# Linear attention and a mixture of experts in one kernel: the running state enters the key-value products through an identity matmul

## The chip, the cores and the metric

One core of one Trainium2 chip. The metric is the device time of one execution in microseconds (us). The kernel before takes 488.33 us in the median of three runs.

## The reference

For 4 sequences of 768 tokens and 8 heads of 48, a gated linear attention runs token by token: the state S of 48 x 48 is scaled row-wise by alpha and gets the outer product of k and v; the output is q times S. The 384 outputs of a token go through one of 8 experts (384 to 1024 to 384). Which one depends on a gate: a token takes its own best expert, or keeps that of the token before it.

```python
state = alpha[:, :, t, :, None] * state + np.einsum('bhd,bhe->bhde', k[:, :, t], v[:, :, t])
y[:, :, t] = np.einsum('bhd,bhde->bhe', q[:, :, t], state)
...
fresh_e = int(np.argmax(logits[b, s]))
e = fresh_e if (s == 0 or local_gate[b, s] < 0.5) else prev_e
h = np.maximum(x[b, s] @ w1[e], 0.0)
out[b, s] = p[e] * (h @ w2[e])
```

All is float32. The expert products split each operand into a high and a low part and add three products of one pass each (float32r).

## The kernel before, in words

**Attention in slots.** The tokens make 24 blocks of 128 (two chunks of 64), six for each of the 4 sequences; block i belongs to sequence i % 4. The main loop (L684) has a slot for each block and two slots more. In slot i the pieces of several blocks are issued, and the order of the program is kept on every engine (`pinned`, L658), so that what stands in the code is the order of each queue:

- `one_a(i+2)` and `scan2(i+1)`: GpSimd sets four ones in a; VectorE scans a backwards (tile sf), GpSimd scales k by it (x<-x,sf).
- `kt(i)`: TensorE transposes k (kp), ScalarE copies it (kk). `copies(i-1)`: ScalarE copies the states of both chunks (st) into the padded tile sb. `state(i-1)`: VectorE makes the next block's state of that sequence.
- `pm(i)`: 16 small products of k and q (pe); VectorE masks them (pq).
- `scan1(i+2)`: VectorE scans a forwards (A), GpSimd scales q by it (x<-x,A). Then the loads of a and x for block i+3 on SP.
- `xt(i-2)`: transposes the outputs (xp, copy xx) for the router. `ym(i-1)`: outputs from pq and v, and from q and sb (y), copy XR, store to xd; then `load_v(i+2)`.
- `first_v(i+1)`: ScalarE copies the first chunk's values beside a block of zeros in vt, so that one product gives both chunks' key-value sums.
- `um(i)`: eight products of kk and vt (up, four heads' pairs on two column groups); VectorE adds the state to both chunks' sums, PSUM to SBUF (L387). For the first four blocks the state is filled with zeros by GpSimd (L375).

Three times in a slot `other()` (L622) runs the deferred VectorE work, one step of each router that is under way, and either two products of zeros (`dense(DN)`, tile dz into h) or, once the first three groups are routed, a piece of the early experts' work.

**Routing** (`route`, L432) takes four blocks as a group when they are done. It is a generator: each `yield` ends a step, and an `other()` takes one step. Its pieces on TensorE are lg, lt, rp, rb, pw and lp; between them are small VectorE operations and ScalarE copies. The one-hot of a token's place in a tile (on) is made by eight ScalarE activations, in four steps; for the last group by VectorE at once.

**Experts.** When group 2 has been routed, `early()` (L562) gives out pieces: experts 0 and 1 for the first 1536 tokens, then the rest of expert 1. A piece is a transposition of gathered rows (tp, xh, xl), one first-layer tile (nine products into h, then hh on ScalarE and hl on VectorE; two halves of h2 alternate), or some second-layer products (yp). The weights of experts 0 and 1 are split by ScalarE (w1h, w2h) and VectorE (w1l, w2l) inside the slots. After the slots the remaining jobs run one after the other.

Setup (L647 to L657) fills constants on GpSimd ahead of the first block; further constants come three a slot from the list `made` (L660).

Of the kernel before, what the change touches and what calls it, by code (L numbers as in the profile page):

```python
# [8 lines left out]
F32 = mybir.dt.float32  # L9
# [10 lines left out]
DM = H * D  # L20
# [26 lines left out]
DN = 2  # L47
# [19 lines left out]
def gla_moe(ctx, tc, akq, vw, vn, wg, w1, w2, cst, tok, out):  # L67
# [188 lines left out]
    with ExitStack() as ac, ExitStack() as aa:  # L256
# [16 lines left out]
        for j in range(2):  # L273
            sb = ap.tile([R, 2, 2, CW], F32, bufs=1, name=f"sb{j}")
            g_.memset(sb[0:64], 0.0)
            g_.memset(sb[64:112, :, 1, :], 0.0)
            SBs.append(sb)
            oh = ap.tile([128, E, G + 1], F32, bufs=1, name=f"oh{j}")
            g_.memset(oh, 0.0)
            OHs.append(oh)  # L280

        st = {"c": c0}
        sts = [ap.tile([R, 3, HP, D], F32, tag="st", bufs=G + 1, name=f"st_{i}") for i in range(G)]
# [30 lines left out]

        def first_v(i):
            vt = VTs[i % NP]
            s_.copy(vt[0:64, 0, :], vt[0:64, 1, :])

        def scan1(i):
# [7 lines left out]
            q2 = x[:, BW:].rearrange("p (s t) -> p s t", t=C)  # L327
            g_.tensor_tensor(q2, q2, A.rearrange("p (s t) -> p s t", t=C + 1)[:, :, 1:], ALU.mult)
            d["k"] = x[:, 0:BW].rearrange("p (h t) -> p h t", h=HP)
            d["q"] = x[:, BW:2 * BW].rearrange("p (h t) -> p h t", h=HP)  # L330

# [37 lines left out]
        def um(i):  # L369
# [3 lines left out]
            if i < G:  # L373
                s3 = sts[i]
                g_.memset(s3[:, 0], 0.0)  # L375
            else:
                s3 = st["S", i % G]
            uw = pp.tile([128, 512], F32, tag="up", name=f"up_{i}")
            up = uw[0:R, 0:2 * CW].rearrange("p (h c d) -> p c h d", c=2, h=HP)
            for hp in range(HP):  # L380
                n = slice(2 * hp * D, 2 * (hp + 1) * D)
                t_.matmul(uw[64:112, n], lhsT=kk[:, hp, 64:112], rhs=vt[:, :, 2 * hp * D:(2 * hp + 1) * D],
                          start=True, stop=True)
                t_.matmul(uw[0:64, n], lhsT=kk[:, hp, 0:64], rhs=vt[:, :, (2 * hp + 1) * D:(2 * hp + 2) * D],
                          start=True, stop=True)
            n = 2 if i + G < NB else 1
            v_.tensor_tensor(s3[:, 1:1 + n], up[:, 0:n], s3[:, 0].unsqueeze(1).broadcast_to([R, n, HP, D]), ALU.add)  # L387
            d["s3"] = s3

        def copies(i):  # L390
            sf, sb = blk[i]["s3"].rearrange("p c h d -> p c (h d)"), blk[i]["sb"]
            s_.copy(sb[64:112, :, 0, :], sf[64:112, 0:2])
            s_.copy(sb[0:48, :, 1, :], sf[0:48, 0:2])

        def state(i):
            d = blk[i]
            if i + G < NB:
                sn = ap.tile([R, 3, HP, D], F32, tag="st", bufs=G + 1, name=f"st_{i + G}")
                v_.scalar_tensor_tensor(sn[:, 0], d["s3"][:, 2], 1.0 / SEED,
# [32 lines left out]
        def route(g):  # L432
# [36 lines left out]
            yield  # L469
# [29 lines left out]
            yield  # L499
            v_.tensor_tensor(ex, ex, ob, ALU.mult)  # L500
            pn = rt([128, n], "pn")
            v_.tensor_reduce(pn, ex, AX.X, ALU.add)
            v_.tensor_tensor(pl[:, :, 0], pn, se, ALU.mult)
# [5 lines left out]
            yield  # L509
            ps = rt([128, E, n + 1], "ps")  # L510
# [25 lines left out]
            if end:  # L536
                v_.tensor_tensor(on, iob.unsqueeze(1).broadcast_to([128, n, TS]),
                                 rr.unsqueeze(2).broadcast_to([128, n, TS]), ALU.is_equal)
            else:
                for j in range(n):  # L540
                    s_.activation(on[:, j], iob, AF.Abs, bias=rr[:, j:j + 1], scale=-1.0)
                    s_.activation(on[:, j], on[:, j], AF.Relu, bias=one[:, 0:1], scale=-float(TS))
                    if j < n - 1:
                        yield
# [17 lines left out]
        def early():  # L562
# [10 lines left out]
            for _ in range(4):  # L573
                yield False
# [47 lines left out]
        def other(pieces=True):  # L622
# [5 lines left out]
            if work[0] is None:  # L628
                if DN:
                    dense(DN)  # L630
# [46 lines left out]
        ]  # L677
        one_a(0)
        scan1(0)
        scan2(0)  # L680
        one_a(1)
        scan1(1)
        wsteps = iter(())
# [257 lines left out]
```

## Time and profile before

| what | us |
|---|---|
| three runs | 485.93, 488.33, 488.93 |
| profiled execution | 484.0 |
| its span | 482.2 |
| first key transposes (slot 0) | at 11.25 |
| slot 5, slot 12, slot 17 begin | at 40.63, 88.96, 119.94 |
| first product of the second early job | at 201.30 |

PE is TensorE's products, PEld its weight loads, DVE VectorE, ACT ScalarE, POOL GpSimd, SP the queue that issues most loads. The granted clock is 1.0 at full speed; its mean is 0.961. Nearly every instruction passes through a helper at line 81, so groups are told apart by tile names, not by lines. A float32 product leaves two records, a float32r product or a transposition one.

### The profile page before, as it was taken

What the parts mean: (1) busy time and instruction counts of PE and PEld (TensorE: products, weight loads), DVE (VectorE), ACT (ScalarE), POOL (GpSimd) and SP (SyncE); (2) the same over time, 40 slices, a digit from 0 to 9 for tenths busy, and PEclk for the clock granted to TensorE, in tenths of its full rate; (3) what the DMA queues carried; (4) which work ended last, traced back from release to release, by engine and by line L of the source; (5) the groups of instructions that cost most, each with busy time, mean ns of one, the idle gap of its engine ahead of it and who ended that gap; (6) DMA issues with size and microseconds to landing.
All of it is one profiled execution on the core that took longest, in us unless ns stands there. A gap on an engine that the chain in (4) does not pass through costs nothing.

```text
span 482.2 us, 10873 instructions
## 1 busy us (share of the span) xinstructions
PE 437.9 (91%) x4443; PEld 391.5 (81%) x4443; DVE 257.3 (53%) x485; ACT 194.1 (40%) x390; POOL 186.7 (39%) x207
## 2 busy tenths in 40 slices
PE   5999898999997978698989999999999999999990
PEld 5777776878875877597878998998989989989990
DVE  4778999898997235722274445244254252342310
ACT  1345656565756436321354324335144233242210
POOL 6654326364556000261053642724732503504201
PEclk9799999999998899888899999999999999999997
DMA  8789767596661102660075554444351542531100
GB/s 217 199 260 252 222 187 201 164 292 167 189 208 50 51 17 71 180 186 27 1 224 188 134 181 138 124 131 123 114 175 57 158 130 65 174 98 39 50 3 27
DMA packets 26710, 66.01 MB, mean 137 GB/s; under 512 B 4384, under 2 KB 10677, under 8 KB 26658
## 3 DMA queue, kind: packets, MB, share of 16 engines
q1 hardware_dynamic: 18672, 49.65, 36.3%
q0 software_dynamic: 3840, 10.62, 6.9%
q10 hardware_dynamic: 4146, 5.03, 3.1%
q8 instruction: 35, 0.57, 0.5%
q14 instruction: 17, 0.14, 0.1%
HBM read 55.84 MB, written 10.62 MB: 138 GB/s over the span
## 4 chain that ended last, share of the span: by engine, by line
PE 53%; issue 11%; DVE 9%; ACT 3%; POOL 2%; POOLq 0%; DVEq 0%; ACTq 0%
PE h L81 24%; PE yp L81 20%; PE y L81 3%; PE tp L81 2%; DVE A L81 2%; POOL out L81 1%; PE up L81 1%; DVE st L81 1%; DVE sf L81 1%; DVE pq L81 1%; ACT hh L81 1%; POOL w1l_0b L81 1%; PE pe L81 1%; DVE xl L81 1%; PE lp L81 1%
## 5 line engine op out<-in xcount | busy, mean ns | idle before, releaser
L81 DVE SCALAR_TENSOR_TENSOR hl<-h,hh 128x480 fp32r<-128x480 f32 (+2 forms) x80 | 43.9, 556 | 77.2 <-ACT hh L81 76.9
L81 ACT ACTIVATE hh<-h 128x480 fp32r<-128x480 f32 (+2 forms) x80 | 38.7, 490 | 82.4 <-PE h L81 82.3
L81 POOL DMA_INDIRECT out<-yo,idx x32 | 32.5, 1017 | 80.5 <-DVE yo L81 78.0
L81 POOL DMA_INDIRECT xg<-xd,idx x32 | 32.6, 1018 | 61.0 <-PE tp L81 52.9
L81 DVE TENSOR_SCALAR yo<-yp,acc 128x384 f32<-128x384 f32 (+1 forms) x32 | 19.6, 616 | 61.1 <-PE yp L81 61.0
L81 POOL TENSOR_TENSOR x<-x,sf 112x512 f32<-112x512 f32 x24 | 29.0, 1209 | 42.5 <-DVE sf L81 42.5
L81 POOL TENSOR_TENSOR x<-x,A 112x512 f32<-112x512 f32 x24 | 31.8, 1327 | 29.0 <-DVE A L81 6.6
L81 DVE TENSOR_TENSOR_SCAN A<-a,z 112x520 f32<-112x520 f32 x24 | 34.5, 1437 | 5.6 <-POOL a L81 5.6
L81 PE MATMUL h<-dz 128*128 128x256 f32 x142 | 35.0, 354 | 2.1 <-DVE z L81 2.1
L81 DVE TENSOR_TENSOR_SCAN sf<-a,z 112x520 f32<-112x520 f32 x24 | 33.8, 1408 | 0.1
L81 ACT COPY sb<-st 48x384 f32<-48x384 f32 x48 | 24.5, 510 | 11.5 <-DVE st L81 10.9
L81 PEld LDWEIGHTS h<-dz 128*128 128x128 f32 x142 | 23.8, 224 | 6.5 <-DVE z L81 2.1
L81 PEld LDWEIGHTS y<-vt,pq 64*64 64x64 f32 x768 | 24.9, 138 | 4.0 <-issue 3.8
L81 PE MATMUL y<-vt,pq 64*64 64x48 f32 x768 | 27.9, 224 | 0.0
L81 PE MATMUL y<-sb,x 112*64 112x96 f32 x384 | 21.8, 258 | 4.3 <-ACT sb L81 4.2
L81 PE MATMUL up<-vt,kk 128*48 128x96 f32 (+1 forms) x384 | 23.1, 267 | 0.0
L81 PEld LDWEIGHTS y<-sb,x 112*64 112x64 f32 x384 | 17.2, 140 | 6.2 <-ACT sb L81 5.2
L81 PEld LDWEIGHTS up<-vt,kk 128*48 128x48 f32 (+1 forms) x384 | 18.3, 140 | 3.4 <-issue 1.0
L81 ACT COPY kk<-kp 128x448 f32<-128x448 f32 x24 | 12.8, 531 | 20.7 <-PE kp L81 20.6
L81 PE MATMUL h<-xh,w1h_1a 128*128 128x256 f32 (+1 forms) x48 | 16.4, 342 | 3.9 <-DVE hl L81 2.7
L81 ACT COPY XR<-y 128x384 f32<-128x384 f32 x24 | 11.5, 479 | 20.1 <-PE y L81 20.1
L81 ACT CAST xh<-tp 128x384 fp32r<-128x384 f32 (+1 forms) x32 | 14.0, 462 | 13.9 <-PE tp L81 13.6
(247 smaller groups left out, 1234.8 us busy)
## 6 DMA issues: line engine op xcount, KB each, us to landing
x<-akq SPq DMA_DIRECT2D x24, 448.0 KB, 5.6
a<-akq SPq DMA_DIRECT2D x24, 227.9 KB, 4.5
vt<-vn SPq DMA_DIRECT2D x24, 192.0 KB, 2.7
xd<-XR ACTq DMA_DIRECT2D x24, 192.0 KB, 4.8
rw_0a<-w SPq DMA_DIRECT2D x3, 512.0 KB, 4.9
rw_0a<-w SPq DMA_DIRECT2D x4, 384.0 KB, 4.2
rw_1a<-w SPq DMA_DIRECT2D x3, 512.0 KB, 5.9
rw_1a<-w SPq DMA_DIRECT2D x4, 384.0 KB, 3.5
```

The costliest lines, as they stand in the source:

```text
L81: r = f(*a, **k)
```

## The change

- The state addition on VectorE goes. For blocks from the fifth on, `um` begins with a product of the identity and the state, repeated for both chunks (112 x 112 by 384 columns, float32), and the eight key-value products add to it in the same bank. `copies` takes the first chunk's state from SBUF and the second's straight from PSUM, four copies for two; `state` reads the third from PSUM. The state tiles shrink to a third.
- `first_v` goes; `load_v` loads the first chunk's values a second time, to where the copy put them.
- `copies` and `state` stand ahead of `kt` in a slot.
- Routing: one empty step goes, the product with the chosen expert (eo) goes to GpSimd, two VectorE operations move a step on, and the one-hot is made by VectorE in one operation for all groups: 11 steps for 15.
- Zeros: `other()` issues one product by default and two at its first call in a slot, four a slot for six. `early()` waits two calls instead of four between gather and transposition.
- Setup: of the fills ahead of the first block five stay on GpSimd; the rest go into `made`, five a slot. The scaling of q of block 0 stands behind that of k. c0 and c1 are worked out from ioa.

```diff
-DN = 2
+DN = 1
...
-        sts = [ap.tile([R, 3, HP, D], F32, tag="st", bufs=G + 1, name=f"st_{i}") for i in range(G)]
+        sts = [ap.tile([R, HP, D], F32, tag="st", bufs=G + 1, name=f"st_{i}") for i in range(G)]
...
-        def first_v(i):
-            vt = VTs[i % NP]
-            s_.copy(vt[0:64, 0, :], vt[0:64, 1, :])
+            y_.dma_start(VTs[i % NP][0:64, 0, :], vn[0:64, at * DM:(at + 1) * DM])
...
-            g_.tensor_tensor(q2, q2, A.rearrange("p (s t) -> p s t", t=C + 1)[:, :, 1:], ALU.mult)
+            d["A"] = A
+            if i:
+                scale_q(i)
...
+        def scale_q(i):
+            q2 = blk[i]["x"][:, BW:].rearrange("p (s t) -> p s t", t=C)
+            g_.tensor_tensor(q2, q2, blk[i].pop("A").rearrange("p (s t) -> p s t", t=C + 1)[:, :, 1:], ALU.mult)
...
-            if i < G:
-                s3 = sts[i]
-                g_.memset(s3[:, 0], 0.0)
-            else:
-                s3 = st["S", i % G]
             uw = pp.tile([128, 512], F32, tag="up", name=f"up_{i}")
             up = uw[0:R, 0:2 * CW].rearrange("p (h c d) -> p c h d", c=2, h=HP)
+            if i < G:
+                st["S", i] = sts[i]
+                g_.memset(sts[i], 0.0)
+            else:
+                t_.matmul(uw[0:R, 0:2 * CW], lhsT=ident[0:R, 0:R],
+                          rhs=st["S", i % G].unsqueeze(2).broadcast_to([R, HP, 2, D]), start=True, stop=False,
+                          skip_group_check=True)
...
-                          start=True, stop=True)
+                          start=i < G, stop=True, skip_group_check=True)
-            n = 2 if i + G < NB else 1
-            v_.tensor_tensor(s3[:, 1:1 + n], up[:, 0:n], s3[:, 0].unsqueeze(1).broadcast_to([R, n, HP, D]), ALU.add)
-            d["s3"] = s3
+            d["up"], d["S"] = up, st["S", i % G]
...
-            s_.copy(sb[64:112, :, 0, :], sf[64:112, 0:2])
-            s_.copy(sb[0:48, :, 1, :], sf[0:48, 0:2])
+            for c, x in ((0, d["S"]), (1, d["up"][:, 0])):
+                s_.copy(sb[64:112, c, 0], x[64:112])
+                s_.copy(sb[0:48, c, 1], x[0:48])
...
-                v_.scalar_tensor_tensor(sn[:, 0], d["s3"][:, 2], 1.0 / SEED,
+                v_.scalar_tensor_tensor(sn, d["up"][:, 1], 1.0 / SEED,
                                         d["end"].unsqueeze(2).broadcast_to([R, HP, D]), ALU.mult, ALU.mult)
...
-            yield
-            v_.tensor_tensor(ex, ex, ob, ALU.mult)
-            pn = rt([128, n], "pn")
-            v_.tensor_reduce(pn, ex, AX.X, ALU.add)
-            v_.tensor_tensor(pl[:, :, 0], pn, se, ALU.mult)
+            eo = rt([128, n, 8], "eo")
+            g_.tensor_tensor(eo, ex, ob, ALU.mult)
...
+            pn = rt([128, n], "pn")
+            v_.tensor_reduce(pn, eo, AX.X, ALU.add)
+            v_.tensor_tensor(pl[:, :, 0], pn, se, ALU.mult)
...
-            if end:
-                v_.tensor_tensor(on, iob.unsqueeze(1).broadcast_to([128, n, TS]),
-                                 rr.unsqueeze(2).broadcast_to([128, n, TS]), ALU.is_equal)
-            else:
-                for j in range(n):
-                    s_.activation(on[:, j], iob, AF.Abs, bias=rr[:, j:j + 1], scale=-1.0)
-                    s_.activation(on[:, j], on[:, j], AF.Relu, bias=one[:, 0:1], scale=-float(TS))
-                    if j < n - 1:
-                        yield
+            v_.tensor_tensor(on, iob.unsqueeze(1).broadcast_to([128, n, TS]),
+                                              rr.unsqueeze(2).broadcast_to([128, n, TS]), ALU.is_equal)
...
-            for _ in range(4):
-                yield False
+            yield False
+            yield False
...
-            if i < NB:
-                kt(i)
             if 0 < i <= NB:
                 copies(i - 1)
                 state(i - 1)
             if i < NB:
+                kt(i)
+            if i < NB:
                 pm(i)
...
-            for _ in range(min(3, len(made))):
+            for _ in range(min(5, len(made))):
                 made.pop(0)()
-            other(i >= NB)
+            other(i >= NB, 2)
```

On TensorE, slot 4 (the first with a state to add; cs holds the identity, h<-dz are zeros), before:

```order
L81 MATMUL kp_562<-cs,x_310 128x112 x4
L81 MATMUL pe_573<-x_310 64x64 x16
L81 MATMUL h_118<-dz 128x256 x2
L81 MATMUL xp_602<-cs,XR_538 128x128 x3
L81 MATMUL y_607<-vt_98,pq_493 64x48 x16
L81 MATMUL y_607<-sb_109,x_247 64x96 x8
L81 MATMUL h_118<-dz 128x256 x2
L81 MATMUL up_639<-vt_100,kk_567 48x96
L81 MATMUL up_639<-vt_100,kk_567 64x96
```

and now:

```order
L81 MATMUL kp_545<-cs,x_288 128x112 x4
L81 MATMUL pe_552<-x_288 64x64 x16
L81 MATMUL h_114<-dz 128x256 x2
L81 MATMUL xp_586<-cs,XR_518 128x128 x3
L81 MATMUL y_591<-vt_98,pq_471 64x48 x16
L81 MATMUL y_591<-sb_108,x_225 64x96 x8
L81 MATMUL h_114<-dz 128x256
L81 MATMUL up_622<-st_247,cs 112x384
L81 MATMUL up_622<-vt_100,kk_550 48x96
```

One product of zeros behind y is gone (and one behind up), and the identity product with its 384 columns stands ahead of the eight of up.

On VectorE, slot 6 (the pass from one pq to the next; w1l is the low part of a first-layer weight), before:

```order
L81 TENSOR_TENSOR pq_683<-pe_666,cs 128x512
L81 SCALAR_TENSOR_TENSOR A_687<-a_598,z_91 112x520
L81 RECIPROCAL z_92<-A_687 112x4
L81 TENSOR_TENSOR w1l_0a_731<-rw_0a_440,w1h_0a_730 128x1024
L81 TENSOR_TENSOR st_370<-up_751,st_370 112x384
L81 SCALAR_TENSOR_TENSOR sf_768<-a_598,z_92 112x520
L81 SCALAR_TENSOR_TENSOR st_780<-st_370,A_500 112x192
L81 TENSOR_TENSOR pq_799<-pe_782,cs 128x512
```

and now:

```order
L81 TENSOR_TENSOR pq_667<-pe_650,cs 128x512
L81 SCALAR_TENSOR_TENSOR A_673<-a_582,z_91 112x520
L81 RECIPROCAL z_92<-A_673 112x4
L81 TENSOR_TENSOR w1l_0a_717<-rw_0a_419,w1h_0a_716 128x1024
L81 SCALAR_TENSOR_TENSOR sf_752<-a_582,z_92 112x520
L81 SCALAR_TENSOR_TENSOR st_759<-up_736,A_480 112x192
L81 TENSOR_TENSOR pq_785<-pe_768,cs 128x512
```

The addition ahead of the backward scan is gone; the scaling behind the scan reads the bank up itself.

On TensorE, slot 20 behind the transposes of the outputs (pw is routing, w1h and w1l are expert 0's weights), before:

```order
L81 MATMUL y_2448<-vt_100,pq_2327 64x48 x16
L81 MATMUL y_2448<-sb_109,x_1984 64x96 x8
L81 MATMUL pw_2478<-oi_2391,one 128x40
L81 MATMUL pw_2478<-oh_112,trif 128x8x4
L81 MATMUL up_2481<-vt_102,kk_2406 48x96
```

and now:

```order
L81 MATMUL y_2444<-sb_108,x_1977 64x96 x8
L81 MATMUL h_114<-xh_0_2352,w1h_0a_716 128x256
L81 MATMUL h_114<-xl_0_2353,w1h_0a_716 128x256
L81 MATMUL h_114<-xh_0_2352,w1l_0a_717 128x256
L81 MATMUL h_114<-xh_0_2352,w1h_0a_848 128x256
L81 MATMUL h_114<-xl_0_2353,w1h_0a_848 128x256
L81 MATMUL h_114<-xh_0_2352,w1l_0a_849 128x256
L81 MATMUL h_114<-xh_0_2352,w1h_0a_958 128x256
L81 MATMUL h_114<-xl_0_2353,w1h_0a_958 128x256
L81 MATMUL h_114<-xh_0_2352,w1l_0a_959 128x256
L81 MATMUL up_2490<-st_2044,cs 112x384
```

The first tile of the first early job stands in slot 20 now; before, its place was slot 22. Over the whole program TensorE has 142 products of zeros before and 99 now.

51 lines of the change are left out of this document (26 added, 25 removed).

## The prediction

> **What bounds the kernel now.** I read the page first: busy shares of the engines and the row of the granted clock.
>
> ```profile
> span 482.2 us, 10873 instructions
> PE 437.9 (91%) x4443; PEld 391.5 (81%) x4443; DVE 257.3 (53%) x485; ACT 194.1 (40%) x390; POOL 186.7 (39%) x207
> DVE  4778999898997235722274445244254252342310
> PEclk9799999999998899888899999999999999999997
> ```
>
> TensorE is busy 91% of the span, but part of that is zeros, and the shares mix stages. VectorE's digits are 7 to 9 up to the fourteenth slice and low afterwards. So I cut the span where the program changes: the fill, slots 0 to 4, 5 to 11 (the first expert's weights are split here), 12 to 16, 17 up to the second early job's first product, and the rest. Columns are window, its length, busy time of PE, PEld, DVE, ACT, POOL, the clock, DMA share and GB/s.
>
> ```profile
> 0.00:11.25 11.25, 6.41 (x32) 6.20 (x33) 4.68 (x7) 1.80 (x2) 7.78 (x39) 0.98 0.88 213
> 11.25:40.63 29.38, 27.02 (x492) 22.60 (x493) 23.25 (x32) 12.23 (x25) 15.89 (x28) 0.89 0.85 240
> 40.63:88.96 48.33, 43.41 (x833) 36.27 (x832) 43.43 (x82) 29.74 (x66) 21.51 (x24) 0.96 0.68 196
> 88.96:119.94 30.98, 30.20 (x591) 25.48 (x590) 28.27 (x62) 18.64 (x45) 14.28 (x15) 1.00 0.77 226
> 119.94:201.30 81.36, 68.59 (x1045) 58.39 (x1044) 54.22 (x135) 43.70 (x104) 25.51 (x26) 0.96 0.37 107
> 201.30:250.00 48.70, 42.82 (x260) 39.75 (x260) 17.91 (x36) 13.04 (x27) 17.21 (x17) 0.86 0.35 105
> 250.00:482.20 232.20, 219.45 (x1201) 202.82 (x1199) 85.51 (x134) 74.91 (x122) 84.54 (x59) 0.98 0.38 113
> ```
>
> In slots 5 to 16 TensorE and VectorE are both near 90% or more (43.41 and 43.43 of 48.33; 30.20 and 28.27 of 30.98): neither can be relieved alone. In the fifth window TensorE is idle for 12.8 us, so there is time to win. After 250 us nothing of the change is left; I leave 232.2 us as they are.
>
> Idle time is not TensorE's only loss. Four stretches ran at half clock:
>
> ```profile
> 59.50:62.50 3.00, 3.00 (x42) 2.55 (x43) 2.30 (x6) 1.21 (x3) 1.23 (x2) 0.57 0.85 247
> 154.30:161.10 6.80, 6.80 (x71) 6.07 (x69) 1.33 (x8) 2.74 (x7) 1.79 (x2) 0.50 0.20 61
> 202.10:208.90 6.80, 6.08 (x29) 5.61 (x28) 2.38 (x7) 1.15 (x3) 4.83 (x5) 0.51 0.84 245
> 226.10:232.90 6.80, 5.93 (x26) 5.46 (x27) 1.03 (x3) 0.71 (x2) 0.00 (x0) 0.51 0.03 8
> ```
>
> Each costs about half its length where TensorE is the bound: 1.5, 3.4, 3.1 and 3.0 us. These rows show what TensorE waits for (first two columns: start and duration; the bracket is the idle time before):
>
> ```profile
> 151.68 0.53 DVE L81 TENSOR_TENSOR xl<-tp,xh 128x384 fp32r<-128x384 f32 x1
> 152.31 0.57 PE L81 MATMUL kp<-cs,x 112*128 112x112 f32 x4 [1.86 <-issue]
> 169.84 0.38 PE L81 MATMUL h<-xh,w1h_0a 128*128 128x256 f32 x1 [0.78 <-DVE hl L81]
> 192.16 0.22 PE L81 MATMUL rb<-cs,em 32*128 32x32 f32 x1 [1.58 <-DVE em L81]
> 200.42 1.10 PE L81 MATMUL lp<-vo,on 128*128 128x96 f32 x8 [2.50 <-DVE on L81]
> ```
>
> The 1.86 us "issue" ends as VectorE's xl frees the bank that kp needs. All of them wait, at the end, for VectorE: a queue of small work there holds TensorE up, although VectorE's average is only 53%. The closings of the clock follow such waits.
>
> **The change part by part.** Durations of what goes, stays and comes:
>
> ```profile
> L81 DVE TENSOR_TENSOR st<-up,st 112x384 f32<-112x384 f32 x20 | 10.9, 547 | 7.2 <-POOL a L81 3.8 <-PE up L81 1.8 <-POOL st L81 1.5
> L81 DVE TENSOR_TENSOR ex<-ex,oh 128x32 f32<-128x32 f32 x6 | 2.8, 466 | 0.0
> 199.59 0.68 DVE L81 TENSOR_TENSOR on<-iob,rr 128x512 f32<-128x512 f32 x1
> L81 ACT COPY vt<-vt 64x384 f32<-64x384 f32 x24 | 12.3, 512 | 12.3 <-ACT XR L81 8.5 <-DMA vt<-vn 3.9
> L81 ACT ACTIVATE on<-on,one 128x128 f32<-128x128 f32 x20 | 8.0, 402 | 0.6
> L81 ACT COPY sb<-st 48x384 f32<-48x384 f32 x48 | 24.5, 510 | 11.5 <-DVE st L81 10.9
> ```
>
> VectorE loses the state additions (10.9 us for twenty, shorter ones for the last four blocks) and six products with ex (2.8, now on GpSimd); it gains five one-hots of 0.68 us (3.4). Net some -0.5 us a slot. It also loses a place in its queue: the addition waited for um of the same slot and stood ahead of the backward scan, while now only the scaling of the state waits, behind the scan. That scaling now waits for ScalarE's copies too, as both read the same bank; queued behind it on VectorE are pq, for which the next slot's y waits, and the next A, for which GpSimd's scaling of q waits. The backward scan (1.2 us) ahead of it covers the two copies out of the bank. ScalarE loses 12.3 us of copies and 16 us of activations, and its 48 copies become 96 of half the width; by 0.51 us for 384 columns and 0.40 for 128 I take 0.3 to 0.43 each, so +4 to +17 us. It is 60% busy in slots 5 to 16, its copies start as um ends and the first two need no product at all, so I cost this at nothing; were the cover gone, 4 x 0.4 us ahead of kk would hold the transposes xp by about 0.6 us a slot. The second load of the values is 98 KB a block, 24 times, one more issue on SP behind load_v's wait for ym; um needs it two slots later, and DMA stands at 0.68 to 0.85. At nothing, with 1 us against me in slots 0 to 4, where it stands ahead of the next blocks' a and x on SP's queue.
>
> TensorE loses 43 products of zeros (the order of its instructions has 142 before, 99 after) and gains 20 products of 112x112 by 384 columns. The price of one zero product, by slots with the same routing (16 has six, 20 none):
>
> ```profile
> 114.17 0.55 PE L81 MATMUL kp<-cs,x 112*128 112x112 f32 x4
> 119.94 0.45 PE L81 MATMUL kp<-cs,x 112*128 112x112 f32 x3
> 137.09 0.60 PE L81 MATMUL kp<-cs,x 112*128 112x112 f32 x4
> 142.53 0.60 PE L81 MATMUL kp<-cs,x 112*128 112x112 f32 x4 [0.35 <-POOL x L81]
> 2.15 6.41 PE L81 MATMUL h<-dz 128*128 128x256 f32 x32 [2.15 <-DVE z L81]
> ```
>
> 119.94 - 114.17 = 5.77 against 5.44 - 0.35 = 5.09: 0.68 us for six, 0.11 each; the thirty-two at the start take 0.20 each. I take 0.13, nearer to the slots: 43 x 0.13 = 5.6 us (4.7 to 8.6).
>
> The identity product does not occur in the trace. Neighbours in float32 are
>
> ```profile
> L81 PE MATMUL y<-vt,pq 64*64 64x48 f32 x768 | 27.9, 224 | 0.0
> L81 PE MATMUL lg<-xx,wgs 128*32 128x128 f32 x144 | 6.8, 279 | 1.1 <-ACT xx L81 0.9
> 105.46 1.13 PE L81 MATMUL lp<-vo,on 128*128 128x96 f32 x8
> 106.37 0.37 PE L81 MATMUL h<-dz 128*128 128x256 f32 x1
> ```
>
> From 48 to 128 columns one record grows by 55 ns, 0.69 ns a column, and one product leaves two records: 384 columns stream in 0.53 us. That is the low end. The high end is four lp products, which also make 384 columns but load weights four times: 106.37 - 105.46 = 0.91 us. I take 0.70, between them, since weights are loaded once: 20 x 0.70 = +14.0 us (10.6 to 18.2). By the Trainium skill, FP8 and Floating Point Precision (TensorE Precision Notes), true float32 takes four passes; at the warm N / 2.4 of TensorE: Matmul & The Clock Gate (Back-to-back issue gap) that would be an estimate of 0.64 us and a term of 12.8 us.
>
> So TensorE has 14.0 - 5.6 = 8.4 us more to do, and only saved waits can make the kernel faster. By stage:
>
> Start, slots 0 to 4: -2.2. The a-memset of block 0 no longer stands behind 28 other fills, and the scaling of q is put behind that of k.
>
> ```profile
> 6.34 1.24 DVE L81 TENSOR_TENSOR_SCAN A<-a,z 112x520 f32<-112x520 f32 x1 [4.23 <-POOL a L81]
> 7.83 2.11 DVE L81 TENSOR_TENSOR_SCAN sf<-a,z 112x520 f32<-112x520 f32 x1
> 30.57 0.56 DVE L81 TENSOR_TENSOR st<-up,st 112x384 f32<-112x384 f32 x1 [1.28 <-POOL a L81]
> ```
>
> The first scan waits 4.23 us, but its data land only shortly before, and then pe waits for q: I take -0.7 (0 to -2). In slots 1 to 4 the state addition waits 1.28 us for the fill of the state, queued behind q's scaling; after it follow sf, the scaling, pq and the next A. Now the fill holds up ScalarE's copies instead and the scan goes ahead: about 0.4 us a slot, -1.5 (-2.5 to +1).
>
> Slots 5 to 11: fourteen zeros less, -1.8; seven identities, +4.9; idle 4.9 to 2.0 with VectorE 3.5 us lighter, -2.9; half of the first closing, -0.8. Sum -0.6. Slots 12 to 16: eleven zeros less, -1.4, five identities, +3.5, next to no idle time to win, -0.2: +1.9.
>
> Slot 17 to 201.30: eight zeros less, -1.0; seven identities, +4.9; lp of the third group, now over by slot 16, -0.9. The early experts' work now enters at slot 19, not 21, and the eight first-layer tiles run two a slot in slots 20 to 23, where one waits under scans and not for the previous tile's hl. Idle 12.8 to 7.0, -5.8: the waits of the 169.84 kind go and the last group's routing has one step less; em and on stay. The closing at 154.30 goes in half of the cases, -1.7. Sum -4.5. After 201.30: the closing at 202.10 in half of the cases, -1.6.
>
> Sum: -2.2 - 0.6 + 1.9 - 4.5 - 1.6 = -7.0 us. The profiled execution took 484.0 us (span 482.2 and 1.8 around it), which gives 477.0; the runs shown have a median of 488.33, 4.3 above it, so for a median I say 481.3.
>
> **The rivals.** (1) Larger gain: the identity costs 0.53 (-3.4), the closings at 59.50, 154.30 and 202.10 all go (-4.0 more): -14.4, 474. For it: the closings follow waits for VectorE. Against: the tp, xl, kp wait of 1.86 us is still in the program.
>
> (2) The idle time stays, because it is latency of chains and not VectorE's load: half of the waits counted as saved (4.5 of 8.9) and the closings (4.1) remain: +1.6, 490, no change. For it: em and on wait on five steps across three engines.
>
> (3) The clock closes more often, as each slot has two zeros fewer. Price 3.4 us a closing; three more make -7.0 + 10.2 = +3.2, 491.5, no change. For it: the closing at 154.30 followed waits that were each under 2 us. Against: the products in their place keep TensorE as busy. The Trainium skill says in TensorE: Matmul & The Clock Gate (Why this matters for your kernels) that gaps above some 3 us between bursts close it; by that rule the zeros in the slots are idle weight and this rival is void. The 1.86 us ahead of 154.30 does not agree with it.
>
> (4) Slower: TensorE is the bound wherever it counts. Identity at 0.91 (+18.2), zeros at 0.11 (-4.7), lp -0.9, start -2.2, no wait or closing saved: +10.4, 498.7. For it: 30.20 of 30.98 in slots 12 to 16. Its place is um in slots 4 to 23; it decides if, at 0.91, fewer than 5.5 us of waits are saved.
>
> **How the numbers follow.** Forecast 40%, rival 1 22%, rival 2 22%, rival 3 7%, rival 4 9%. About 1% (4.9 us) is what a measurement of this kernel tells from no change. Forecast and rival 1 are faster: 0.62; rivals 2 and 3 no change: 0.29; rival 4 slower: 0.09. The range reaches from rival 1's 474 to rival 2's 490; outside it lie rivals 3 and 4 (16%) and what is beyond. The likeliest case alone covers 477 to 485, by 10.6 to 18.2 for the identities.
>
> **What would show it.** Right: a group up<-st with two records a product and 0.6 to 0.8 us between its start and that of the next up; slots 12 to 16 taking 32 to 34 us; VectorE idle in them; first-layer tiles at slot 20; the second early job starting near 190; 250 us onwards unchanged. Wrong: slots 5 to 16 longer than 84 us, more half-clock stretches than four, waits for em and on larger than before, or ScalarE's copies as the releaser of xp.

## The result and the profile after

The changed kernel takes 504.49 us in the median of four runs (502.06 to 507.48), the kernel before 488.19 on the same chip: ratio 1.0345, 95% interval 1.0275 to 1.0414. It is slower by 3.4%; the forecast was 481.3 us, and 504.49 lies above the range. The profiled executions took 507.48 and 484.0 us, so this pair differs by 23.5 us where the medians differ by 16.3: the windows below show more of a loss than the medians do.

The page of the changed kernel, to be read against the rows of before:

```profile
span 505.7 us, 10886 instructions
PE 455.5 (90%) x4440; PEld 398.7 (79%) x4440; DVE 244.9 (48%) x462; ACT 177.8 (35%) x374; POOL 184.6 (36%) x200
DVE  4785875777658331672237333525335244252410
PEclk9598997999988798977989999999999999999997
```

VectorE and ScalarE have less to do, as forecast (244.9 for 257.3, 177.8 for 194.1 us). TensorE is 17.6 us busier, and the clock row has more drops. Where the time went is told by windows cut at the same places of the program: slots 0 to 4, slots 5 to 19, slot 20 up to the first product of expert 2, the rest. Columns as in the prediction. First after, then the two of before that were not cut so there:

```profile
8.94:41.04 32.10, 28.50 (x484) 22.89 (x485) 24.88 (x32) 10.91 (x28) 19.21 (x42) 0.84 0.88 242
41.04:159.58 118.54, 103.28 (x1782) 80.59 (x1781) 82.30 (x169) 52.92 (x136) 48.72 (x61) 0.93 0.67 191
159.58:274.70 115.12, 98.40 (x948) 86.57 (x948) 50.40 (x124) 38.42 (x89) 28.67 (x30) 0.88 0.29 89
274.70:505.70 231.00, 218.92 (x1198) 202.52 (x1198) 83.54 (x132) 74.24 (x121) 83.99 (x59) 0.99 0.37 112
```

```profile
40.63:137.09 96.46, 90.29 (x1775) 75.77 (x1774) 88.02 (x178) 60.22 (x140) 46.58 (x51) 0.98 0.71 206
137.09:251.24 114.15, 95.16 (x949) 84.25 (x950) 56.98 (x139) 45.74 (x103) 31.93 (x30) 0.91 0.32 95
```

Slot 0 begins 2.3 us earlier (8.94 for 11.25) and slots 0 to 4 give 2.7 back; from expert 2 on both take 231.0 us. Slots 5 to 19 take 118.54 for 96.46: 22.1 of the 23.5 us of span stand there, 13.0 of them as TensorE's busy time (103.28 - 90.29) and 9.1 as its waits (15.26 - 6.17).

The waits of TensorE in those slots, grouped by who was waited for (total us, times, longest). After:

```profile
PE xp L81 <- ACT kk L81: 4.1, 5, 1.5
PE lp L81 <- POOL a L81: 3.7, 2, 1.8
PE pw L81 <- DVE se L81: 3.0, 2, 1.7
PE lp L81 <- DVE on L81: 2.7, 1, 2.7
PE kp L81 <- issue: 1.2, 1, 1.2
```

Before:

```profile
PE rp L81 <- DVE acc L81: 2.0, 2, 1.5
PE lt L81 <- ACT lc L81: 1.7, 3, 0.8
PE y L81 <- ACT sb L81: 1.5, 2, 1.1
PE rb L81 <- DVE em L81: 0.4, 1, 0.4
```

With 0.4 us of rb the waits after make 15.1 us, those before 5.6. Nearly all of them are of two kinds that before did not have: the routing's products pw and lp (9.4 us), and the transposes xp, which wait until ScalarE has read the bank for kk. Two of them on the timelines of the changed kernel (start, duration; the bracket is the idle time before). VectorE ahead of pw:

```profile
63.97 1.22 DVE L81 TENSOR_TENSOR w1l_0a<-rw_0a,w1h_0a 128x1024 fp32r<-128x1024 f32 x1 [1.28 <-ACT w1h_0a L81]
65.11 0.23 DVE L81 TENSOR_TENSOR_SCAN oi<-m,oh 128x40 f32<-128x40 f32 x1
65.26 0.16 DVE L81 TENSOR_REDUCE se<-ex 128x4 f32<-128x32 f32 x1
```

GpSimd ahead of lp of the next group:

```profile
104.50 1.70 POOL L81 TENSOR_TENSOR x<-x,A 112x512 f32<-112x512 f32 x1 [2.80 <-issue]
106.17 0.83 POOL L81 TENSOR_TENSOR vo<-oa,vals 128x384 f32<-128x384 f32 x1
```

TensorE at those two places:

```profile
62.12 0.81 PE L81 MATMUL up<-st,cs 112*112 112x384 f32 x2
62.86 0.88 PE L81 MATMUL up<-vt,kk 128*48 128x96 f32 x16
65.49 0.39 PE L81 MATMUL pw<-oi,one 128*128 128x40 f32 x2 [1.75 <-DVE se L81]
...
103.58 0.81 PE L81 MATMUL up<-st,cs 112*112 112x384 f32 x2
104.32 0.88 PE L81 MATMUL up<-vt,kk 128*48 128x96 f32 x16
107.04 1.13 PE L81 MATMUL lp<-vo,on 128*128 128x96 f32 x8 [1.85 <-POOL a L81]
```

oi takes 0.23 us, but it stands behind a weight split that waits 1.28 us for ScalarE's cast, and its product pw comes one step later. At 107.04 the one-hot on is long done; lp waits for vo, which stands on GpSimd behind the scaling of q, and that behind VectorE's scan A. (The row names a, GpSimd's small fill after vo.) Before, pw came two steps after oi, and lp four after vo. The same rows show the identity's price: 62.86 - 62.12 = 0.74 us, and again 104.32 - 103.58.

Behind such waits the clock closes. Three of the stretches after:

```profile
75.50:82.30 6.80, 6.80 (x99) 5.74 (x101) 3.69 (x6) 1.16 (x3) 2.41 (x3) 0.51 0.17 44
137.00:143.80 6.80, 6.80 (x99) 5.20 (x89) 4.88 (x6) 1.47 (x4) 5.73 (x5) 0.50 0.49 126
161.00:167.90 6.90, 6.90 (x62) 5.60 (x60) 4.22 (x14) 1.34 (x3) 2.60 (x3) 0.51 0.42 117
```

They begin 1 to 2 us after the 2.7 us wait of lp (ended at 74.40), the 1.84 us wait of lp at 135.16, and the 1.2 us wait of kp at 159.58.

### The profile page after: what moved, and what is told of

The parts are those of the page before. It is cut to its first block, busy times and chain, and to the rows that moved or that the text cites. A ratio compares the mean times of both kernels' runs of the same rounds, so it can differ in the third digit from the quotient of the medians.

```text
span 505.7 us, 10886 instructions
## 1 busy us (share of the span) xinstructions
PE 455.5 (90%) x4440; PEld 398.7 (79%) x4440; DVE 244.9 (48%) x462; ACT 177.8 (35%) x374; POOL 184.6 (36%) x200
## 4 chain that ended last, share of the span: by engine, by line
PE 67%; issue 12%; ACT 7%; DVE 6%; POOL 3%; DMA 3%; ACTq 0%; POOLq 0%; SPq 0%; DVEq 0%
PE h L81 24%; PE yp L81 20%; PE y L81 10%; PE up L81 4%; ACT sb L81 3%; PE xp L81 2%; DMA vt<-vn 2%; PE tp L81 2%; PE lp L81 1%; PE pe L81 1%; PE lg L81 1%; POOL x L81 1%; POOL out L81 1%; PE kp L81 1%; ACT kk L81 1%
## 5 line engine op out<-in xcount | busy, mean ns | idle before, releaser
L81 DVE TENSOR_TENSOR_SCAN A<-a,z 112x520 f32<-112x520 f32 x24 | 32.8, 1366 | 6.2 <-POOL a L81 6.2
L81 PEld LDWEIGHTS y<-vt,pq 64*64 64x64 f32 x768 | 28.2, 153 | 4.6 <-issue 4.6
L81 PE MATMUL y<-vt,pq 64*64 64x48 f32 x768 | 31.4, 238 | 0.0
L81 PE MATMUL h<-dz 128*128 128x256 f32 x99 | 28.2, 375 | 2.1 <-DVE z L81 2.1
L81 PE MATMUL y<-sb,x 112*64 112x96 f32 x384 | 26.2, 287 | 0.1
L81 PEld LDWEIGHTS h<-dz 128*128 128x128 f32 x99 | 18.1, 231 | 6.3 <-DVE z L81 2.1
L81 ACT COPY sb<-st 48x192 f32<-48x192 f32 x48 | 16.8, 350 | 16.1 <-POOL a L81 10.7
L81 PEld LDWEIGHTS y<-sb,x 112*64 112x64 f32 x384 | 20.7, 161 | 1.9 <-ACT sb L81 0.3
L81 PE MATMUL up<-vt,kk 128*48 128x96 f32 (+1 forms) x384 | 21.8, 257 | 0.0
L81 PE MATMUL xp<-cs,XR 128*128 128x128 f32 x72 | 13.6, 301 | 8.4 <-ACT kk L81 8.2
```

The lines of the kernel that those rows point to most:

```text
L81: r = f(*a, **k)
```

## The experiments

Ratios are to the kernel before on the same chip, with the 95% interval. "Slots 5 to 19" is read from each profile, cut as above; lost clock is a window's length times (1 - granted clock), taken in pieces of 0.5 us.

### First round: one part of the change undone

The old routing in the changed kernel:

```diff
+            yield
...
-            eo = rt([128, n, 8], "eo")
-            g_.tensor_tensor(eo, ex, ob, ALU.mult)
+            yield
+            v_.tensor_tensor(ex, ex, ob, ALU.mult)
...
+                for j in range(n):
+                    s_.activation(on[:, j], iob, AF.Abs, bias=rr[:, j:j + 1], scale=-1.0)
```

> The changed kernel with only the routing as it was before (15 steps, the one-hot by eight ScalarE activations in four steps, the product with ex on VectorE). Theory R (the shorter routing makes TensorE wait for VectorE: the waits of pw, rb and lp in slots 5 to 19 add up to 9.7 us against 4.1 before, and the closings of the clock at 75.5 and 137 follow two of them): about 5.5 us of waits and 3.4 to 5 us of half clock go, 494 to 497 us against 504.5. Theory I (the identity products are the loss): no change, 503 to 506. Theory Z (two zeros fewer a slot let the clock close): no change, 503 to 506. Theory K (copies ahead of the key transposes): no change.

Measured: 1.0278 [1.0221, 1.0334]; slots 5 to 19 take 103.5 us for 118.5, no closing in them. Theory R holds for these slots. But the total gains less, since the first early job then begins a slot later and slot 20 up to expert 2 takes 122.3 for 115.1.

Six zeros a slot:

```diff
-DN = 1
+DN = 2
```

> The changed kernel with six products of zeros in a slot again. Theory Z (fewer zeros let the clock close): the seven closings that the profile of before did not have go, 11.8 us of lost clock against 43 x 0.13 = 5.6 us of zeros: 497 to 500 us. Theories R, I and K (the clock closes because of waits, and zeros are TensorE work on the path): 505 to 510 us, with as many closings.

Measured: 1.0413 [1.0338, 1.0489], eight closings between 10 and 260 us where there were nine; no gain. Theory Z falls.

The state added on VectorE:

```diff
-                t_.matmul(uw[0:R, 0:2 * CW], lhsT=ident[0:R, 0:R],
...
+            v_.tensor_tensor(s3[:, 1:1 + n], up[:, 0:n], s3[:, 0].unsqueeze(1).broadcast_to([R, n, HP, D]), ALU.add)
```

> The changed kernel with the state added on VectorE as before (no identity product, the states in SBUF, two wide copies for four). Theory I (TensorE is the bound in slots 4 to 23, an identity takes 0.74 us): 20 x 0.74 = 14.8 us go, less what VectorE's additions (10.9 us) put back into the waits: 490 to 496 us. Theories R and K (the loss is in waits): under 4 us go, 500 to 505 us, and the waits of lp and pw grow, since VectorE has more in its queue.

Measured: 1.0581 [1.0478, 1.0684]: slower than the change itself, which neither theory expected. TensorE has 11 us less to do in slots 5 to 19, but 25.6 us of clock are lost there for 8.5. Theory I falls: the identity products are not the loss. The waits in these slots are 16.0 us, hardly more than the 15.1 of the change, but two closings last 27.3 and 17.1 us, where none of the change's there lasts over 6.8. What keeps them so long no run takes apart.

The key transposes ahead of the copies:

```diff
+            if i < NB:
+                kt(i)
             if 0 < i <= NB:
                 copies(i - 1)
                 state(i - 1)
-            if i < NB:
-                kt(i)
```

> The changed kernel with the key transposes and their copy kk ahead of the four copies of the state, as before. Theory K (ScalarE's copies ahead of kk hold the transposes xp): xp's waits of 4.1 us in slots 5 to 19 go and the closing at 44.5 with them (1.7 us): 497 to 500 us. Rival: the products with sb then wait for the copies instead (1.5 us of such waits before), so the waits change their name: 502 to 505 us.

Measured: 1.0481 [1.0434, 1.0528]. xp's waits for kk go, as theory K says, but lp's grow from 6.4 to 11 us, in the row

```profile
PE lp L81 <- POOL a L81: 11.0, 3, 4.1
```

and slots 5 to 19 take 126.1 us. The wait has moved, to a dearer place than the rival thought. That VectorE's scaling of the state now waits for copies behind kk, and the scan A and vo with it, fits the order of the queues; no run takes it apart.

### Second round: the routing's half, the second load, two parts alone

The one-hot of the first five groups back on ScalarE in the changed kernel:

```diff
-            v_.tensor_tensor(on, iob.unsqueeze(1).broadcast_to([128, n, TS]),
...
+                for j in range(n):
+                    s_.activation(on[:, j], iob, AF.Abs, bias=rr[:, j:j + 1], scale=-1.0)
...
+                    if j < n - 1:
+                        yield
```

> The changed kernel with only the one-hot of the first five groups back on ScalarE, in four steps (14 steps; the other pieces of the new routing stay). Theory R1 (the one-hot stands on VectorE behind the split of the weights and a scan, and lp waits for it): lp's waits of 2.65, 1.84 and 1.85 us in slots 5 to 19 go and with them the two closings that follow (6.8 us at half clock's loss), 492 to 497 us, about as with all of the old routing. Theory R2 (fewer steps make each piece meet VectorE sooner, pw and rb too): pw's waits of 1.72 and 1.24 us and some closings stay, 499 to 503 us. If the routing is not the loss: 503 to 506.

Measured: 1.058 [1.0495, 1.0666]. lp no longer waits in slots 5 to 19 and these take 111.0 us; pw's 3.0 us stay and xp's grow to 5.7. Slot 20 to the second early job's first product takes 74.8 us for 63.0, with a wait of 4.6 us for lp of the last group. So the 7.5 us won in slots 5 to 19 are lost behind them: another engine for the one-hot alone is no cure, and R1 misses by 4 to 5% (its 492 to 497 us are 1.008 to 1.018 of 488.19).

The second load undone in the changed kernel (`first_v` and its call back, for the added transfer):

```diff
-            y_.dma_start(VTs[i % NP][0:64, 0, :], vn[0:64, at * DM:(at + 1) * DM])
+        def first_v(i):
+            vt = VTs[i % NP]
+            s_.copy(vt[0:64, 0, :], vt[0:64, 1, :])
```

> The changed kernel with the first chunk's values copied by ScalarE again and no second load. Theory V (the second load stands on the chain, the profile's chain gives vt<-vn 2%, some 10 us): 494 to 500 us. Rival (the wait is hidden, and ScalarE's 24 copies of 0.51 us come back ahead of the casts that VectorE's splits wait for): 503 to 508 us, with longer waits of xp for kk or of lp.

Measured: 1.0446 [1.034, 1.0553]. Theory V falls, though the chain of waits names vt<-vn.

Only the new routing in the kernel before (the first diff the other way round, and two empty steps less in `early`):

```diff
-            for _ in range(4):
-                yield False
+            yield False
+            yield False
```

> The kernel before with only the new routing (11 steps, the one-hot on VectorE) and the two empty steps less in the early job. Theory R (the routing costs by itself): waits of lp and pw as in the changed kernel, 5 to 6 us more in slots 5 to 19, and one or two closings more, though six zeros a slot are kept: ratio to before 1.015 to 1.03. Rival (the routing only hurts beside the identity and the copies from PSUM): within 1%.

Measured: 1.0469 [1.0384, 1.0553], more than theory R asked for. Slots 5 to 19:

```profile
40.77:164.48 123.71, 107.68 (x1776) 90.54 (x1774) 89.63 (x188) 53.91 (x119) 47.24 (x58) 0.80 0.60 171
```

TensorE's waits there:

```profile
PE pw L81 <- DVE se L81: 3.1, 2, 1.7
PE lp L81 <- POOL a L81: 2.9, 1, 2.9
PE rb L81 <- DVE em L81: 2.7, 2, 1.5
PE lp L81 <- DVE on L81: 2.7, 1, 2.7
```

27.2 us more than before in these slots, of which some 10 are waits; the clock stands at 0.80 for 0.98, with six zeros a slot. The new routing, here with the two steps of the early job, costs by itself no less than the whole change.

Only the identity in the kernel before (`um`, `copies`, `state` and the states' tiles as in the change):

```diff
+                t_.matmul(uw[0:R, 0:2 * CW], lhsT=ident[0:R, 0:R],
...
+            for c, x in ((0, d["S"]), (1, d["up"][:, 0])):
+                s_.copy(sb[64:112, c, 0], x[64:112])
```

> The kernel before with only the states added through the identity product, four copies for two and the third state read from PSUM. Theory I (TensorE is the bound, each identity 0.74 us): 14.8 us more on TensorE, little of it given back by VectorE's 10.9 us: ratio 1.02 to 1.03. Rival (as where the addition was put back on VectorE in the changed kernel, the products keep the clock and free VectorE): 0.985 to 1.0.

Measured: 0.9956 [0.9923, 0.999]. Slots 5 to 19, and the waits in them:

```profile
42.29:142.72 100.43, 97.81 (x1806) 77.72 (x1804) 84.16 (x164) 65.71 (x172) 47.51 (x52) 1.00 0.71 204
```

```profile
PE rb L81 <- DVE em L81: 1.1, 2, 0.8
PE rp L81 <- DVE acc L81: 0.8, 1, 0.8
PE kp L81 <- POOL x L81: 0.2, 1, 0.2
PE lt L81 <- ACT lc L81: 0.2, 1, 0.2
```

The rival holds. Fifteen identities add 11.1 us, and the slots are 4.0 us longer: the waits fall from 5.6 to 2.3 us and no closing is left.

### Third round: halves of the routing; zeros and order beside the identity

All four start from the kernel before; the last two have the identity too. The one-hot on VectorE:

```diff
-                for j in range(n):
-                    s_.activation(on[:, j], iob, AF.Abs, bias=rr[:, j:j + 1], scale=-1.0)
...
+            v_.tensor_tensor(on, iob.unsqueeze(1).broadcast_to([128, n, TS]),
```

> The kernel before with the one-hot of all groups on VectorE in one step (three steps less, nothing else). Theory R1 (the one-hot stands on VectorE behind a weight split and a scan, and lp waits for it): one wait of 2 to 3 us a group in groups 0 to 2, each with a closing of the clock behind it: ratio 1.015 to 1.03. Theory R2 (it is the steps ahead of it, rb and pw, that come too early): within 1%.

Measured: 1.0358 [1.0302, 1.0414]; lp waits three times, 7.8 us in all, for vo on GpSimd. The rest of the new routing, the one-hot on ScalarE:

```diff
-            yield
...
-            yield
-            v_.tensor_tensor(ex, ex, ob, ALU.mult)
...
+            g_.tensor_tensor(eo, ex, ob, ALU.mult)
```

> The kernel before with the rest of the new routing alone: the empty step and the step of the product with ex gone, that product on GpSimd, two VectorE operations behind pw; the one-hot stays on ScalarE in four steps. Theory R2: waits of rb (0.8 to 1.5 us) and pw (1.3 to 1.7 us) in groups 0 and 1, with the closings behind them (58 to 72 and 99 to 113 in the run with all of the new routing): ratio 1.02 to 1.035. Theory R1: within 1%.

Measured: 1.0378 [1.0324, 1.0431]; pw waits 4.8 us, rb 2.7, rp 2.3, and the slots lose 15.4 us of clock. Each half costs by itself, about as much as the whole change: R1 and R2 each expect a loss from their own half, a little less of it than was measured (up to 1.03 and 1.035), and are wrong in expecting none from the other.

Four zeros a slot:

```diff
-DN = 2
+DN = 1
...
-            other(i >= NB)
+            other(i >= NB, 2)
```

> The kernel before with the states through the identity and four products of zeros a slot for six. If zeros are only work on TensorE once no wait is left in slots 5 to 19 (2.4 us of idle time and no closing there with the identity alone): 43 x 0.13 = 5.6 us less, ratio 0.98 to 0.988. Theory Z (zeros hold the clock open): closings come back in slots 5 to 19, ratio 0.995 to 1.015.

Measured: 0.9979 [0.9931, 1.0026], the same as the identity alone within the intervals. In the profiled execution slots 5 to 19 lose no clock, which speaks against theory Z. It does not settle it: that execution (481.86 us) is the second fastest of ten with a median of 484.14, their granted clock is 0.955 to 0.975 for 0.961 to 0.986 with the identity alone (on another chip), and the ratio lies in theory Z's range. In the profile the slots are shorter by the zeros' price:

```profile
41.23:139.69 98.46, 95.24 (x1778) 74.80 (x1777) 84.64 (x165) 65.92 (x172) 48.84 (x52) 1.00 0.72 210
```

With 26 zeros fewer than with the identity alone (two a slot in slots 5 to 17) these slots are 1.97 us shorter: 0.08 us each.

The copies and the state ahead of the key transposes:

```diff
-            if i < NB:
-                kt(i)
             if 0 < i <= NB:
                 copies(i - 1)
                 state(i - 1)
+            if i < NB:
+                kt(i)
```

> The kernel before with the states through the identity, and the copies and the scaling of the state ahead of the key transposes. Theory K (four copies ahead of kk on ScalarE hold xp for 0.5 to 1.3 us a slot, as in the profile of the changed kernel and of that with the old routing): 7 to 15 us more, ratio 1.01 to 1.03. Rival (the copies would hold y otherwise, so the wait only moves): 0.99 to 1.0.

Measured: 1.0168 [1.0111, 1.0225]. Theory K:

```profile
PE xp L81 <- ACT kk L81: 5.4, 10, 1.3
```

Ten waits, most of 0.4 to 0.6 us, and after them slots 5 to 19 take 107.7 us for 100.4. With the old routing the order costs 2.1%.

### Last rounds: distance, and what is left

Three empty steps more in the changed routing, nothing moved to another engine:

```diff
             st["E"] = em[:, 127:128]
             yield
+            yield
...
             g_.tensor_tensor(eo, ex, ob, ALU.mult)
             yield
+            yield
```

> The changed kernel with three empty steps more in the routing, one each between VectorE's result and the product that reads it (ahead of rb, pw and lp); the one-hot stays on VectorE, the copies stay ahead of the key transposes. Theory D (what costs is the distance between a VectorE result and its product, not which engine makes it): the waits of rb, pw and lp (9.7 us in slots 5 to 19) and the closings behind them go; xp's waits stay: ratio to before 1.02 to 1.03, as with the old routing (1.028). Theory L (the one-hot's 0.7 to 1.3 us on VectorE, ahead of the scans, is the cost): 1.035 to 1.045.

(The third stands ahead of lp.) Measured: 1.0227 [1.0151, 1.0303]. Slots 5 to 19, with no closing:

```profile
45.04:147.25 102.21, 96.00 (x1776) 74.50 (x1775) 83.00 (x163) 50.84 (x132) 46.14 (x55) 1.00 0.72 210
```

The waits that are left there:

```profile
PE xp L81 <- ACT kk L81: 3.5, 7, 1.1
PE lt L81 <- DVE acc L81: 1.7, 3, 1.0
PE rp L81 <- DVE kr L81: 1.0, 1, 1.0
```

Theory D holds here: three steps in which the routing does nothing shorten these slots by 16.3 us.

The old routing and the old order together (the edits of the first and the fourth experiment):

```diff
+            if i < NB:
+                kt(i)
             if 0 < i <= NB:
                 copies(i - 1)
...
+            v_.tensor_tensor(ex, ex, ob, ALU.mult)
```

> The changed kernel with the two named causes undone: the routing as before and the key transposes ahead of the copies. What stays of the change: states through the identity, the second load, four zeros a slot, the setup, two empty steps less in the early job. If routing and order are the whole loss: ratio 0.985 to 1.0. If the second load or the setup is a third cause: 1.01 to 1.02.

Measured: 1.0121 [1.0076, 1.0166]; slots 5 to 19 take 98.6 us, but slot 20 up to expert 2 takes 118.8. One wait stands out there. TensorE:

```profile
145.54 0.55 PE L81 MATMUL tp<-cs,xg 128*128 128x128 f32 x3
149.34 0.98 PE L81 MATMUL kp<-cs,x 112*128 112x112 f32 x4 [3.25 <-issue]
```

and VectorE:

```profile
147.56 1.23 DVE L81 TENSOR_TENSOR_SCAN sf<-a,z 112x520 f32<-112x520 f32 x1
148.71 0.53 DVE L81 TENSOR_TENSOR xl<-tp,xh 128x384 fp32r<-128x384 f32 x1
```

The first expert's transposition, brought forward, is issued at the end of a slot whose VectorE queue still holds a router's tail and the scan; kp needs its bank.

The second load, and the setup, each beside the identity in the kernel before:

```diff
-            s_.copy(vt[0:64, 0, :], vt[0:64, 1, :])
+            y_.dma_start(VTs[i % NP][0:64, 0, :], vn[0:64, at * DM:(at + 1) * DM])
```

> The kernel before with the states through the identity and the second load of the values for ScalarE's copy. Theory V (the second load delays the values or the next a and x on SP's queue): 1.005 to 1.02. Rival (the load is hidden; ScalarE's 12.3 us are off the path too): 0.99 to 1.0, as with the identity alone (0.996).

Measured: 0.9967 [0.9916, 1.0019]: the load is hidden.

```diff
-        g_.memset(one, 1.0)
...
+            lambda: g_.memset(one, 1.0),
...
+        scale_q(0)
...
-            for _ in range(min(3, len(made))):
+            for _ in range(min(5, len(made))):
```

> The kernel before with the states through the identity and the new setup (five fills ahead of the first block, five of the list a slot, q of block 0 scaled after k). Theory S1 (the first slot begins 2.3 us earlier and that stays): 0.988 to 0.993. Theory S2 (the fills in the slots hold the scaling of x and the loss comes back in slots 1 to 4 with the clock's closing there, as in the changed kernel, which was level again in slot 4): 0.995 to 1.003.

Measured: 0.9973 [0.9935, 1.0011]: slot 0 begins 2.3 us earlier, slot 5 0.9 us, the end shows nothing. S2.

The two steps of the early job back, beside the old routing and order:

```diff
-            yield False
-            yield False
+            for _ in range(4):
+                yield False
```

> The changed kernel with the old routing, the key transposes ahead of the copies, and the two empty steps in the early job put back. Theory E (two steps less put the first transposition tp at the end of slot 20, where kp waits 3.25 us for xl behind the backward scan, and the clock closes twice behind it, 8.5 us up to the second early job): ratio 0.98 to 0.995, against 1.012 without the two steps. If the loss that is left lies in the second load, the zeros or the setup together: 1.005 to 1.015.

Measured: 0.9985 [0.995, 1.002], for 1.0121 without the two steps. With routing, order and these two steps undone nothing of the loss is left, and nothing is won either. The ratio came out just above what theory E gave; kp's wait is 1.2 us there for 3.25.

The change kept whole, with an empty step ahead of rp, rb, pw and lp, the two steps of the early job, and the key transposes first:

```diff
+            yield

             rp = pp.tile([8 * n, 2, 128], F32, tag=RT, name=f"rp_{g}")
...
+            if i < NB:
+                kt(i)
             if 0 < i <= NB:
                 copies(i - 1)
```

> The whole change kept, with the one-hot on VectorE and the product with ex on GpSimd, but an empty step ahead of rp, rb, pw and lp, two more in the early job, and the key transposes ahead of the copies. Theory D with K and E: no wait over 1 us in slots 5 to 19 and no closing there, ratio 0.98 to 0.995. If the one-hot on VectorE or the number of steps costs by itself: 1.005 to 1.02.

Measured: 1.0177 [1.0114, 1.024]. Theory D misses: lp still waits, three times.

```profile
PE lp L81 <- POOL a L81: 5.7, 3, 2.0
```

GpSimd ahead of the first of these waits:

```profile
73.94 1.99 POOL L81 TENSOR_TENSOR x<-x,A 112x512 f32<-112x512 f32 x1 [2.69 <-issue]
75.88 1.28 POOL L81 TENSOR_TENSOR vo<-oa,vals 128x384 f32<-128x384 f32 x1
```

lp starts at 77.22, as vo ends. Here the step that issues vo falls behind the scaling of q, in the run with three empty steps it fell ahead of it. So it is not a number of steps that protects a product, but what stands in the queues ahead of its producers when the step comes. No version here is clearly faster than the kernel before; the identity alone comes nearest, 0.4% below it.

## Why the prediction was wrong

**The step that failed** is the one on idle time: "idle 4.9 to 2.0 with VectorE 3.5 us lighter, -2.9" in slots 5 to 11, and "Idle 12.8 to 7.0, -5.8: the waits of the 169.84 kind go and the last group's routing has one step less; em and on stay." It took the waits as a matter of VectorE's load and the routing's change as one more or one fewer operation there (five one-hots of 0.68 us). The steps taken out (16 pieces became 11, counted with the last one: five steps, not four) were distance: pw two steps behind oi, lp four behind vo. Without them the latency of a queue, VectorE's or GpSimd's, comes out at TensorE. In slots 5 to 19 the waits are 15.1 us for 5.6. That a lighter VectorE shortens waits was right where the routing keeps its distance: 5.6 to 2.3 us with the identity alone. Rival 2 had named the mechanism, latency of chains and not VectorE's load, but let the idle time stay where it grew.

**The clock.** Forecast was half of three closings saved, -4.1. In slots 5 to 19 alone 118.54 x 0.07 = 8.3 us are lost for 96.46 x 0.02 = 1.9. Rival 3 had the right price and the wrong cause: the closings follow the waits, not the missing zeros (with six zeros a slot the changed kernel still had eight closings of nine; four beside the identity brought none back in the profiled execution).

**ScalarE's order.** "I cost this at nothing; were the cover gone, 4 x 0.4 us ahead of kk would hold the transposes xp by about 0.6 us a slot." The cover was gone. Beside the old routing that is 2.1%, by waits of just this size.

**The early job.** That its tiles begin at slot 20 came true (164.85 us) and was counted as a gain. Its two empty steps were not priced: 1.4% beside the old routing and order.

**Right terms.** The identity: 0.74 us for 0.70. The second load: nothing. After 250 us: nothing changed. VectorE's load fell as worked out. The zeros were priced at 0.13 us and are worth 0.08 where they could be measured. The sum by stage left out ten zeros and one identity of slots 0 to 4, -1.3 and +0.7 us at its own prices, which changes nothing. The start came 2.3 us earlier for 0.7, but slots 0 to 4 gave 2.7 back where 1.5 more were to be won.

**Rival 4** ended at 498.7, nearest to the result, for a reason that is not it: TensorE as the bound, with dear identities. The kernel with the identity alone has all of its 14.8 us and is not slower.

**The signs of being wrong** named there all came: slots 5 to 16 take 95.1 us (limit 84), nine closings of the clock between 10 and 260 us for five, waits for em and on of up to 1.75 and 2.68 us for 1.58 and 2.50, and kk's copy on ScalarE as the releaser of xp. Of the signs of being right, the second early job began at 222.6, not near 190.

The parts do not add up: routing 4.7% (with the early steps), order 2.1% and early steps 1.4%, each measured beside another neighbour, against 3.4% together. One wait often covers another, and a closing covers a stretch whatever began it. How much of the 3.4% belongs to each in the changed kernel itself stays open, and so does why it does better with its order of copies than without.

## What to carry to other kernels

An empty step in a hand-made order is a distance between a producer and its consumer: before taking one out, read on each engine what stands ahead of the producer, not how long the producer takes. Price a wait of TensorE of 1 us or more at its own length plus the clock that it may close; here that was some 1.8 us more on average, and shorter waits close together can do the same. An extra product that relieves the queue TensorE waits for can be free, and taking load off an engine does not shorten a wait that is a chain.

## What the runs showed of the hardware

**The clock closes behind short waits.** In the twenty profiles, between 38 and 255 us, TensorE waited 177 times for 1.0 us or more, with the clock open as the wait began. In 98 of the cases a closing began during the wait or within 4 us of its end: 44 of 88 for waits of 1.0 to 1.5 us, 18 of 41 up to 2 us, 36 of 48 above; for 0.6 to 1.0 us in 14 of 124. Per wait of 1.0 us or more that is 324.3 / 177 = 1.83 us of lost clock. The count does not part neighbouring waits, and a wait alone does not decide: nearly half close nothing. The Trainium skill, TensorE: Matmul & The Clock Gate (Why this matters for your kernels), asks for no gaps above some 3 us; these runs do not agree, since nearly all waits counted here are shorter than that.

Most of what decides stands in the records of the clock. Up to the last change in each of the twenty profiles, every stretch of open clock (1.0) or half clock (0.5) lasts a multiple of 3.41 us (3.41, 6.83, 10.24 and so on). On that grid, the open pieces of 3.41 us between 38 and 255 us sort by the time in them without a product, all waits together: with less than 1.0 us, none of 880 was followed by half clock; with 1.0 to 2.0 us, 64 of 154; with more, all 32. That makes all 96 closings there. In 17 pieces the 1.0 us was reached without any single wait that long, and 11 of them closed. In the changed kernel the piece from 72.20 to 75.61 us has 2.20 us without a product, and the clock closes at its end; the 1.85 us wait that ends at 107.04 is cut by a border at 106.33 into 1.13 and 0.72 us and closes nothing. A closed piece with 0.6 us or more without a product was always followed by another closed one (39 of 39); with less, 55 of 147 were.

**VectorE and GpSimd hold each other up.** In the last experiment x<-x,A on GpSimd and two VectorE operations overlap. GpSimd's two rows stand above (1.99 and 1.28 us); VectorE's are

```profile
73.93 0.94 DVE L81 TENSOR_TENSOR w2l_0a<-rw_0a,w2h_0a 128x768 fp32r<-128x768 f32 x1
74.79 1.68 DVE L81 TENSOR_TENSOR on<-iob,rr 128x512 f32<-128x512 f32 x1
```

on takes 0.66 to 0.68 us where GpSimd does not stand in its way (0.68 in the prediction's row), and vo 0.83 in the row at 106.17. Here on is 1.0 us longer, with 1.1 us of x<-x,A left as it began, and vo 0.45 us longer, with 0.6 us of on left. The Trainium skill, SBUF — State Buffer (SBUF: two separate sides), says that one of the two takes a shared pair of ports for a whole instruction while the other waits; the rows agree.
